# Turning P and dS: two sets of 64x64 products against one set of stacked K=128 products

## The chip, the cores and the metric

The kernel runs on one core of one Trainium2 chip. The metric is the device time of one execution in microseconds (us). Times are medians over several executions, with the lowest and highest; all runs named "fast" had a mean granted TensorE clock of 0.997 to 1.0 of full speed. "Slow" for this one-core program means over 1.5% above the fastest run of the same kernel. The experiments ran in three sets, each on another chip; the kernel before ran along in each.

## The reference

Forward and backward of window attention: 1024 windows of 8x8 = 64 tokens, 384 channels, one head of width 384.

```python
qkv = xw @ wqkv                                   # xw: 1024 windows x 64 x 384
p = softmax(einsum('bqc,bkc->bqk', q, k) * scale)  # P, 64 x 64 per window
o = einsum('bqk,bkc->bqc', p, v) @ wo
# returned: o and, for a given grad_out, the gradients of x, wqkv and wo
```

The backward pass needs dS, the gradient of the scores, and both P and dS also in transposed form.

## The kernel before

Work goes by "quads": 4 tiles of 128 tokens, each tile two windows, one in partitions 0 to 63 (LO) and one in 64 to 127 (HI). 128 quads make a software pipeline; in one step TensorE works on three of them. All PSUM tiles come from one ring of 8 banks, handed out in turn, so that a tile waits until the tile of eight hand-outs ago has been evicted.

```python
ring = ctx.enter_context(tc.tile_pool(name="ring", bufs=8, space=bass.MemoryType.PSUM))
...
def turn(st, kind):                 # kind 0: P -> PT, kind 1: dS -> ST
    n = ("PT", "ST")[kind]
    st[n] = dst = qp.tile([P, QUAD, WT], BF16, tag=n, name=n)
    pt = ring.tile([P, QUAD, WT], F32, tag="r", name="pt")
    for t in range(QUAD):
        for w, o, h in ((0, LO, HI), (1, HI, LO)):
            lhs, h = (st["Pb"][o, t, :], o) if kind == 0 else (st["ps"][h, w, t, :], h)
            nc.tensor.matmul(pt[o, t, :], lhsT=lhs, rhs=ident[h, h], start=True, stop=True)
    nc.vector.tensor_copy(out=dst[:], in_=pt[:])
...
def attend(st, pair, after=None):
    ...
    for t in pair:
        po, pu, pw, pd = [ring.tile([P, C], F32, tag="r", name=n) for n in ("po", "pu", "pw", "pd")]
        both((pu, "ST", "xq", True), (po, "PT", "uq", True))    # 4 products 64x64x384
        # osb <- po on ScalarE, Uq <- pu on VectorE
        both((pw, "Pb", "dq", True), (pd, "ST", "vq", False))   # 4 products 64x64x384
        # Wq <- pw on VectorE
        made.append((t, pd))
        store(out_0, osb, bp, t0 + t)
    if after is not None:
        turn(after, 0)
        turn(after, 1)
    for t, pd in made:
        for w, o in ((0, HI), (1, LO)):                          # K=128, M=64
            nc.tensor.matmul(pd[o, :], lhsT=st["ps"][:, w, t, :], rhs=st["tok"][:, :, t, w, :], start=False, stop=True)
        dsb = ob.tile([P, C], BF16, tag="d")                     # ob: 4 buffers of each kind
        # dsb <- pd on ScalarE, then store to out_1
```

A step (cut to the engine order of TensorE): scores, eight `uv` products, projection 0, one group `pg` of 12 weight-gradient products, `attend(c, (2, 3), b)` with the turn of quad b in it, projection 1 (its first products read `A_sb`), another `pg`, `attend(b, (0, 1))`. The matrix `ps` holds, for each tile and window, P in one half of the partitions and dS in the other: the stationary of the `pd` products. `xT`, `dT` and `tok` are transposed copies that DMA makes (of `x`, of the given gradient, and of the projections); their transposes are issued by SyncE, the loads of the gradient (`dq`) and the stores of `osb` and `dsb` by GpSimd, on one queue (q0 on the page, 151.68 MB).

## Time and profile before

| | before |
|---|---|
| time, median of the runs of the first comparison | 2078.51 us (2078.35 to 2081.12, 4 runs) |
| TensorE busy | 99% of the span |
| VectorE, ScalarE, GpSimd busy | 67, 71, 68% |
| turn products; their PSUM copies | 2048; 256 of 415 ns each |

Three lines of the profile page of the kernel before: the span, the busy time of the engines (us, share, number of instructions), and the shares by engine of the chain of work that ended last.

```profile
span 2076.4 us, 51332 instructions
PE 2057.4 (99%) x18814; PEld 1116.9 (54%) x18814; DVE 1391.1 (67%) x3235; ACT 1469.8 (71%) x3213; POOL 1418.0 (68%) x2566
...
PE 97%; DMA 2%; DVE 1%; ACT 0%; issue 0%
```

So only what shortens TensorE's stream shortens the kernel. The list of TensorE's waits in the same trace (total us, times, longest us) suggests that nothing is to be had from waits:

```profile
PE pt L74 <- DMA w_sb<-in_wqkv_dram: 6.5, 1, 6.5
PE pj L147 <- DMA dT<-dq: 2.2, 3, 1.0
PE pd L263 <- DMA tok<-yz: 1.7, 3, 0.8
```

That list is blind to short waits: a product of 384 columns is shown as 320 to 350 ns long, while the next of a plain sequence starts 162 ns after it. A wait of up to about 190 ns (350 less 162) fits under the bar of the product before. One has to look at starts. The timeline of one step of the kernel before, from the second tile's attention products to projection 1 (start us, duration us, engine, line, operation, shapes, count; weight loads and a few other lines left out):

```profile
1007.00 0.86 ACT L252 CAST osb<-po 128x384 bf16<-128x384 f32 x2 [0.16 <-ACT yz L150]
1007.06 0.32 PE L245 MATMUL pw<-dq,Pb 64*64 64x384 bf16 x1
1007.13 0.55 DVE L253 CAST Uq<-pu 128x384 bf16<-128x384 f32 x1
1007.27 0.35 PE L245 MATMUL pd<-vq,ST 64*64 64x384 bf16 x2
1007.28 0.35 PE L245 MATMUL pw<-dq,Pb 64*64 64x384 bf16 x1
1007.53 0.31 PE L230 MATMUL pt<-ident,Pb 64*64 64x64 bf16 x8
...
1007.74 0.31 PE L230 MATMUL pt<-ident,ps 64*64 64x64 bf16 x8
...
1007.98 0.52 PE L263 MATMUL pd<-tok,ps 128*64 128x384 bf16 x4
...
1008.42 0.82 PE L147 MATMUL pj<-xT,A_sb 128*128 128x512 bf16 x3
```

From the last attention product (1007.28) to the first turn product are 0.25 us instead of 0.16; the single instructions of the trace give 248 ns, and 42 ns before that start stands a semaphore update of ScalarE, some 10 ns after the end of the first `osb` copy (1006.995 + 0.479 = 1007.474). The second turn (1007.74) follows 42 ns after the update that comes, again some 10 ns late, with the end of the `Uq` copy (1007.133 + 0.548 = 1007.681). Both waits are for PSUM banks: the two turns take the banks of the first `po` and the first `pu`. Neither shows in TensorE's wait list, though they take 88 ns (248 less 160) and 61 ns of a step (the second turn starts 90 ns after the pair before it, where pairs follow after about 30). Over all steps the same lag of 42 ns repeats at the 5th, 25th and 50th percentile, as it must where that wait is the last to end. The start must also be later than the normal distance allows, as it is here (248 ns instead of about 160).

### The profile page before, as it was taken

To read this page: it belongs to the slowest core of one execution; us is meant where nothing else is said; L and a number is where in the kernel's file an instruction comes from. 1 tells how busy PE (TensorE), PEld (TensorE's weight loads), DVE (VectorE), ACT (ScalarE), POOL (GpSimd) and SP (SyncE) were. 2 spreads that over 40 slices of the span, in tenths; PEclk is the share of its full clock that TensorE was granted. 3 is DMA by queue.
4 is the path that set the end of the run, shared out by engine and by line. 5 is a ranking of instruction groups with operands and counts; after the bars stand their busy time and mean duration, and the time that the engine had idled before them with its cause. 6 is when DMAs were issued, how large, how long until landed. Compare 5 with 4: busy or idle time off the path is not lost.

```text
span 2076.4 us, 51332 instructions
## 1 busy us (share of the span) xinstructions
PE 2057.4 (99%) x18814; PEld 1116.9 (54%) x18814; DVE 1391.1 (67%) x3235; ACT 1469.8 (71%) x3213; POOL 1418.0 (68%) x2566
## 2 busy tenths in 40 slices
PE   8999999999999999999999999999999999999998
PEld 4455555555555555555555555555555555555554
DVE  5666666666666666666666666666666666666665
ACT  5767777777777777777777777677777777777773
POOL 4766766767667767667676766676767677666764
PEclk9999999999999999999999999999999999999999
DMA  9999999999999999999999999999999999999992
GB/s 203 222 210 199 200 200 197 213 197 199 199 197 201 201 201 201 200 197 201 199 198 197 205 199 194 198 209 194 203 199 203 203 192 202 199 200 198 201 172 77
DMA packets 997181, 409.06 MB, mean 197 GB/s; under 512 B 880704, under 2 KB 971584, under 8 KB 996928
## 3 DMA queue, kind: packets, MB, share of 16 engines
q1 hardware_dynamic: 873648, 253.80, 72.1%
q0 software_dynamic: 122880, 151.68, 30.7%
q8 instruction: 147, 2.41, 0.5%
q14 instruction: 106, 0.87, 0.1%
q10 hardware_dynamic: 400, 0.29, 0.0%
HBM read 101.84 MB, written 101.84 MB: 98 GB/s over the span
## 4 chain that ended last, share of the span: by engine, by line
PE 97%; DMA 2%; DVE 1%; ACT 0%; issue 0%
PE pg L278 24%; PE pj L147 24%; PE pj L219 23%; PE pd L263 5%; PE pu L245 5%; PE sd L165 5%; PE pw L245 4%; PE pd L245 3%; PE pt L230 3%; DMA tok<-yz 1%; DMA dT<-dq 0%; PE pc L96 0%; DMA w_sb<-in_wqkv_dram 0%; PE pe L369 0%; PE po L245 0%; PE pt L74 0%
## 5 line engine op out<-in xcount | busy, mean ns | idle before, releaser
L235 POOL DMA_DIRECT2D out_dram<-osb x1024 | 576.2, 569 | 432.0 <-ACT osb L252 338.1
L235 POOL DMA_DIRECT2D out_dram<-dsb x1024 | 570.6, 563 | 133.9 <-DMA dq<-in_grad_out_dram 38.8
L280 DVE TENSOR_TENSOR GF_acc<-pg,GF_acc 128x384 f32<-128x384 f32 x258 | 144.0, 558 | 489.1 <-PE pg L278 489.1
L278 PEld LDWEIGHTS <-xq 128*128 128x128 bf16 x3072 | 300.3, 98 | 225.4 <-issue 0.9
L219 PEld LDWEIGHTS <-xT 128*128 128x128 bf16 x3072 | 291.8, 98 | 182.2
L252 ACT CAST osb<-po 128x384 bf16<-128x384 f32 x512 | 220.9, 483 | 233.5 <-PE pu L245 162.3
L219 PE MATMUL pj<-B_sb,xT 128*128 128x384 bf16 x1536 | 333.4, 326 | 0.0
L219 PE MATMUL pj<-AT_sb,xT 128*128 128x384 bf16 x1536 | 333.3, 326 | 0.0
L118 POOL DMA_DIRECT2D dq<-in_grad_out_dram x512 | 273.8, 549 | 71.6 <-PE pj L147 27.3
L221 ACT CAST uq<-pj 128x384 bf16<-128x384 f32 x512 | 247.3, 483 | 74.4 <-PE pj L219 70.1
L253 DVE CAST Uq<-pu 128x384 bf16<-128x384 f32 x512 | 280.6, 548 | 8.4 <-PE pu L245 8.4
L266 ACT CAST dsb<-pd 128x384 bf16<-128x384 f32 x512 | 220.7, 482 | 89.6 <-PE pd L263 68.5
L255 DVE CAST Wq<-pw 128x384 bf16<-128x384 f32 x512 | 280.6, 548 | 0.0
L147 PE MATMUL pj<-dT,BT_sb 128*128 128x512 bf16 x1152 | 269.6, 379 | 2.2 <-DMA dT<-dq 2.2
L147 PE MATMUL pj<-xT,A_sb 128*128 128x512 bf16 x1152 | 270.8, 380 | 0.0
L278 PE MATMUL pg<-Uq,xq 128*128 128x384 bf16 x1536 | 270.4, 326 | 0.0
L278 PE MATMUL pg<-Wq,xq 128*128 128x384 bf16 x1536 | 270.0, 326 | 0.0
L221 ACT CAST vq<-pj 128x384 bf16<-128x384 f32 x512 | 250.0, 488 | 2.4
L152 ACT CAST yz<-pj 128x512 bf16<-128x512 f32 x384 | 224.7, 585 | 16.8
L245 PE MATMUL pw<-dq,Pb 64*64 64x384 bf16 x1024 | 227.2, 329 | 0.2
L198 ACT COPY ps<-Pb 64x256 bf16<-64x256 bf16 x256 | 103.3, 403 | 149.8 <-DVE Pb L195 148.3
L245 PEld LDWEIGHTS <-ST 64*64 64x64 bf16 x2048 | 119.9, 105 | 161.6 <-issue 148.5
(65 smaller groups left out, 2501.6 us busy)
## 6 DMA issues: line engine op xcount, KB each, us to landing
xq<-in_x_dram SPq DMA_DIRECT2D x512, 96.0 KB, 4.0
dq<-in_grad_out_dram POOLq DMA_DIRECT2D x512, 96.0 KB, 5.3
out_dram<-osb POOLq DMA_DIRECT2D x1024, 48.0 KB, 4.1
out_dram<-dsb POOLq DMA_DIRECT2D x1024, 48.0 KB, 4.0
dT<-dq SPq DMA_TRANSPOSE x128, 6.3
xT<-xq SPq DMA_TRANSPOSE x128, 7.3
tok<-yz SPq DMA_TRANSPOSE x128, 8.0
w_sb<-in_wqkv_dram SPq DMA_DIRECT2D x1, 864.0 KB, 5.7
```

The costliest lines, as they stand in the source:

```text
L118: nc.gpsimd.dma_start(out=dq[:, t, :], in_=dram_tile(grad_out, bp, t0 + t))
L147: nc.tensor.matmul(pj[:].rearrange("p t w k -> p (t w k)"), lhsT=wgt[:, m, mo * P:(mo + 1) * P], rhs=src[:, :, m, :], start=(m == 0), stop ...
L152: ENG[EV["y"][mo]](out=yz[:, mo, :, 1:3, :], in_=pj[:])
L219: nc.tensor.matmul(pj[:], lhsT=st["xT"][:, t, m, :], rhs=wgt[:, m, :], start=(m == 0), stop=(m == CK - 1))
L221: cp(out=dst[:, t, :], in_=pj[:])
L235: nc.gpsimd.dma_start(out=dram_tile(dst, bp, t)[WIN * w:WIN * (w + 1)], in_=src[h, :])
L245: nc.tensor.matmul(dst[o, :], lhsT=st[lhs][h, t, :], rhs=st[rhs][h, t, :], start=True, stop=done)
L252: ENG[EV["o"][t]](out=osb[:], in_=po[:])
L253: ENG[EV["U"][t]](out=st["Uq"][:, t, :], in_=pu[:])
L255: ENG[EV["W"][t]](out=st["Wq"][:, t, :], in_=pw[:])
L266: ENG[EV["d"][t]](out=dsb[:], in_=pd[:])
L278: nc.tensor.matmul(pw[:], lhsT=st["xq"][:, t, ma * P:(ma + 1) * P], rhs=st["UW"[f] + "q"][:, t, :], start=(i == 0), stop=(i == n - 1))
```

## The change

Both matrices lie stacked in `ps`, over all 128 partitions. One product of K=128 with the full 128x128 identity turns both at once and writes P-transposed and dS-transposed side by side: 8 products of 64x128 per quad instead of 16 of 64x64, one bank instead of two, one copy instead of two. The turn also moves behind the `pd` products, which work in the same 128x64 form.

```diff
--- before.py
+++ after.py
@@ -220,15 +220,19 @@
                              start=(m == 0), stop=(m == CK - 1))
         cp(out=dst[:, t, :], in_=pj[:])
 
-    def turn(st, kind):
-        n = ("PT", "ST")[kind]
-        st[n] = dst = qp.tile([P, QUAD, WT], BF16, tag=n, name=n)
-        pt = ring.tile([P, QUAD, WT], F32, tag="r", name="pt")
+    def turn(st):
+        pt = ring.tile([P, QUAD, 2, WT], F32, tag="r", name="pt")
         for t in range(QUAD):
-            for w, o, h in ((0, LO, HI), (1, HI, LO)):
-                lhs, h = (st["Pb"][o, t, :], o) if kind == 0 else (st["ps"][h, w, t, :], h)
-                nc.tensor.matmul(pt[o, t, :], lhsT=lhs, rhs=ident[h, h], start=True, stop=True)
+            for w, h in ((0, LO), (1, HI)):
+                nc.tensor.matmul(pt[h, t, :, :].rearrange("p s k -> p (s k)"), lhsT=st["ps"][:, w, t, :],
+                                 rhs=ident[:], start=True, stop=True)
+        st["PS"] = dst = qp.tile([P, QUAD, 2, WT], BF16, tag="PS", name="PS")
         nc.vector.tensor_copy(out=dst[:], in_=pt[:])
+
+    def turned(st, n, t, h):
+        if n in ("PT", "ST"):
+            return st["PS"][h, t, int((n == "ST") == (h == LO)), :]
+        return st[n][h, t, :]
 
     def store(dst, src, bp, t):
         for h, w in ((LO, 1), (HI, 0)):
@@ -242,7 +246,7 @@
         def both(straight, crossed):
             for h, o, (dst, lhs, rhs, done) in ((LO, LO, straight), (LO, HI, crossed), (HI, LO, crossed),
                                                 (HI, HI, straight)):
-                nc.tensor.matmul(dst[o, :], lhsT=st[lhs][h, t, :], rhs=st[rhs][h, t, :], start=True, stop=done)
+                nc.tensor.matmul(dst[o, :], lhsT=turned(st, lhs, t, h), rhs=st[rhs][h, t, :], start=True, stop=done)
 
         made = []
         for t in pair:
@@ -255,9 +259,6 @@
             ENG[EV["W"][t]](out=st["Wq"][:, t, :], in_=pw[:])
             made.append((t, pd))
             store(out_0, osb, bp, t0 + t)
-        if after is not None:
-            turn(after, 0)
-            turn(after, 1)
         for t, pd in made:
             for w, o in ((0, HI), (1, LO)):
                 nc.tensor.matmul(pd[o, :], lhsT=st["ps"][:, w, t, :], rhs=st["tok"][:, :, t, w, :], start=False,
@@ -265,6 +266,8 @@
             dsb = ob.tile([P, C], BF16, tag="d")
             ENG[EV["d"][t]](out=dsb[:], in_=pd[:])
             store(out_1, dsb, bp, t0 + t)
+        if after is not None:
+            turn(after)
 
     fill = []
 
@@ -317,8 +320,7 @@
         if c is not None:
             attend(c, (2, 3), b)
         else:
-            B(turn, 0)
-            B(turn, 1)
+            B(turn)
         for mo in range(CK):
             A(project, 1, mo)
         A(to_tokens)
```

## The prediction

> **What bounds the kernel.** TensorE's instruction stream. The page gives PE busy 99% at a full granted clock and 97% of the chain that ended last; DVE, ACT and POOL are at 67 to 71%. PE's wait list has only some 14 us. But matmul ends are modelled and overlap, so short waits count as "busy"; starts of single instructions show them. Products of N=384 follow each other after 162 ns, of N=512 after 216 ns. [...]

> **The part that changes**, once a step, 127 steps, medians or means of the trace, from the last start of the attention group to the first A_sb product:
> - attention to first turn product: 245 ns, where about 160 is normal. It starts 42 ns after a ScalarE semaphore update: the eviction of the first `po`, whose PSUM bank it reuses. About 88 ns lost.
> - first turn to second: 217 ns for eight products that take about 150 (pairs 30 ns apart). The second starts 42 ns after a VectorE update (`Uq` eviction of `pu`). About 61 ns lost.
> - second turn to `pd` products: 242 ns, 93 of it the change from 64x64 to 128x64 tiles.
> - `pd` to A_sb: 448 ns (two pairs 187 ns apart, the last followed after 258 = 163 + 95 for the change to the full array).
> Sum 1152 ns. [...]

> **After.** The number of mode changes stays (64x64, 128x64, full); the turn now runs in the 128x64 mode behind `pd`.
> - attention to `pd`: 277 ns, as before's other attention half shows.
> - `pd` to the turn: 190 + about 162 = 352 ns. No bank wait: the one bank was evicted some 0.4 us earlier.
> - turn: 8 products of N=128. The `pd` products show that the two column halves run as a pair (starts 3 to 4 ns apart)[...], plus 95 for the mode change: 319 ns.
> Sum 948 ns, so 0.20 us less a step, 26 us in all. Of that about 150 ns a step is the two bank waits, the rest fewer instructions.

> **Off the critical path.** VectorE: two copies of 415 ns become one; from 384 columns at 548 and 256 at 415, about 680 ns, so 19 us less in total, worth nothing. The banks that the next projection takes (`pu`, `pw`, `pd`) are evicted in time. The 56 ns wait of the second tile's `pd` for the GF_acc addition stays. DMA is nearly always busy, but its transposes land a median 9 to 12 us before use; at most 1 to 2 us of new DMA waits.

> **Prediction:** 2053 us (1.2% less), range 2046 to 2064. Faster by over 2%: 0.02; within 2%: 0.96; slower: 0.02.

> **What would show it.** Turn products 1024 instead of 2048[...]; no 90 ns gap with a 42 ns lag behind a semaphore; attention to A_sb about 0.95 us; VectorE about 20 us less busy.

> **What would make it wrong.** If the two column halves do not overlap when both stream the same identity, [...]the gain vanishes to about zero. If the bank waits only move (to A_sb's products or the next attention), half the gain goes. If DMA is tighter than its slack suggests, PE waits for `tok` or `dT`.

The sum of the forecast came to 277 + 352 + 319 = 948 ns. What is cut had its source outside the traces, and so had one term of the sum: the 224 ns (319 less 95) for the eight turn products. An estimate from the trace before comes close: products of 512 columns start 216 ns apart and products of 384 columns 162, so 128 columns are worth 54 ns; four pairs are 216 ns, and with 95 for the mode change 311 instead of 319. In the same trace the changes of tiling mode added 93 ns (second turn to `pd`), 95 (`pd` to `A_sb`: 258 less 163) and 115 (attention to `pd`: 277 less 162).

## The result, and the profile after

The changed kernel took 2059.92 us (2058.24 to 2064.11, 4 runs) against 2078.51 us: 18.6 us less. The ratio is 0.9911, with a 95% interval of 0.9893 to 0.9928; ratios are the mean time of one kernel's fast runs over that of the other's of the same rounds, so not quite the ratio of the medians quoted. By the 2% rule that is "same"; the direction is clear. The forecast of 2053 us was 6.9 us too low; the range of 2046 to 2064 held.

The same three lines of the page after the change:

```profile
span 2058.2 us, 49158 instructions
PE 2033.6 (99%) x17790; PEld 1109.3 (54%) x17790; DVE 1381.5 (67%) x3107; ACT 1468.8 (71%) x3213; POOL 1418.4 (69%) x2566
...
PE 93%; DMA 1%; ACT 1%; DVE 1%; POOL 0%; issue 0%; ACTq 0%; POOLq 0%
```

TensorE has 1024 products fewer, VectorE 128 copies fewer, as expected. New is that the chain lies on TensorE for 93% of the span, not 97%, and that the share of ScalarE rose from 0% to 1%. The section that the change rewrites, in the timeline of the changed kernel:

```profile
1002.23 0.35 PE L249 MATMUL pw<-dq,Pb 64*64 64x384 bf16 x1
1002.50 0.52 PE L264 MATMUL pd<-tok,ps 128*64 128x384 bf16 x4
1002.85 0.39 PE L227 MATMUL pt<-ident,ps 128*64 128x128 bf16 x8
1003.17 0.61 PE L147 MATMUL pj<-xT,A_sb 128*128 128x512 bf16 x2
```

Table 1 gives the medians over 126 steps, worked out from the starts of the single instructions (ns after the last attention product's start):

| | first turn product | first `pd` product | first `A_sb` product | predicted |
|---|---|---|---|---|
| before | 248 | 699 | 1147 | (1152 read) |
| after | 626 | 277 | 948 | 948 |

The mean over those steps fell from 1148 to 948 ns, 200 ns, or 25.2 us over 126 steps. **The local part of the forecast (0.20 us a step, 26 us) is right to within 1 us. But the kernel gained only 18.6 us.** The rest must have been given back elsewhere.

To find it, I compared each start-to-start distance on TensorE with the median of its kind and summed what was over by more than 80 ns ("irregular stalls"). Before: 9.4 us, of which 8.3 us in the first 100 us, 1.1 us at the end, none between. After: 16.8 us, of which 9.9 at the start, 1.0 at the end, and 6.0 us between 148 and 211 us, some 5 us of them in one episode from 204 us on. The difference of 7.4 us and the 25.2 us give 2076.4 - 25.2 + 7.4 = 2058.6 us, for a span of 2058.2 us.

The episode in the timeline of the changed kernel: first ScalarE's lines, then TensorE's (brackets: idle time before, and what ended it).

```profile
203.62 0.48 ACT L256 CAST osb<-po 128x384 bf16<-128x384 f32 x1 [2.10 <-DMA out_dram<-osb]
207.27 1.10 ACT L267 CAST dsb<-pd 128x384 bf16<-128x384 f32 x2 [3.18 <-DMA out_dram<-dsb]
```

```profile
204.15 0.65 PE L219 MATMUL pj<-AT_sb,xT 128*128 128x384 bf16 x3 [0.74 <-ACT osb L256]
204.63 0.65 PE L219 MATMUL pj<-B_sb,xT 128*128 128x384 bf16 x3
207.80 1.12 PE L219 MATMUL pj<-AT_sb,xT 128*128 128x384 bf16 x3 [2.52 <-ACT dsb L267]
```

ScalarE cannot write the next output tile, because the stores of its four buffers have not landed: the tile at 207.27 starts 100 ns after the store of the tile four before it landed (207.17). Until then ScalarE shows no other copy (3.18 us idle in the first fence), so banks stay full and TensorE stands still for 2.5 us. That store was late mainly because it was issued late. GpSimd's lines:

```profile
191.57 0.56 POOL L239 DMA_DIRECT2D out_dram<-dsb  x1 [1.79 <-DMA dq<-in_grad_out_dram]
200.43 2.22 POOL L239 DMA_DIRECT2D out_dram<-dsb  x4 [0.25 <-ACT yz L152]
```

The tile was ready at 187.07; its two stores were issued at 200.43 and 200.98, some 14 us later (median over the run: 3.4 us), and the second landed 6.2 us after that (median 4.2). GpSimd had fallen behind while it waited, among others at 191.57 for the landing of a `dq` load that it had issued eight DMAs before. Then comes a second bill, in the windows of the same stretch (us of the window; busy us and number of instructions per engine; granted clock, mean DMA share, GB/s):

```profile
200.00:205.00 5.00, 4.26 (x58) 2.35 (x56) 4.10 (x9) 1.30 (x3) 4.75 (x10) 1.00 1.16 184
205.00:210.00 5.00, 2.48 (x10) 1.05 (x9) 0.00 (x0) 2.56 (x7) 2.85 (x6) 0.74 1.11 249
210.00:215.00 5.00, 5.00 (x27) 2.66 (x26) 3.55 (x9) 3.81 (x10) 4.90 (x10) 0.92 0.96 193
```

The mean granted clock fell to 0.74 and 0.92 of full speed in these windows; products of 384 columns started 320 ns apart instead of 162, eight times in a row. The clock record of the trace shows half speed from 207.36 to 210.78 us. The clock dropped 2.4 us after the start of the last product before the stall (204.96). What makes it drop, and after how long a pause, this one episode does not show.

### The profile page after: what moved, and what is told of

Same layout as the page of the kernel before. It is cut to its first block, busy times and chain, and to the rows that moved or that the text cites. A ratio compares the mean times of both kernels' runs of the same rounds, so it can differ in the third digit from the quotient of the medians.

```text
span 2058.2 us, 49158 instructions
## 1 busy us (share of the span) xinstructions
PE 2033.6 (99%) x17790; PEld 1109.3 (54%) x17790; DVE 1381.5 (67%) x3107; ACT 1468.8 (71%) x3213; POOL 1418.4 (69%) x2566
## 2 busy tenths in 40 slices
DMA packets 997172, 408.92 MB, mean 199 GB/s; under 512 B 880704, under 2 KB 971584, under 8 KB 996928
## 4 chain that ended last, share of the span: by engine, by line
PE 93%; DMA 1%; ACT 1%; DVE 1%; POOL 0%; issue 0%; ACTq 0%; POOLq 0%
PE pg L281 24%; PE pj L147 23%; PE pj L219 23%; PE pd L264 5%; PE pu L249 5%; PE sd L165 5%; PE pw L249 4%; PE pd L249 3%; PE pt L227 1%; DMA out_dram<-dsb 1%; DMA tok<-yz 1%; POOL out_dram L239 0%; ACT uq L221 0%; ACT vq L221 0%; PE pe L371 0%
## 5 line engine op out<-in xcount | busy, mean ns | idle before, releaser
L249 PEld LDWEIGHTS <-PS 64*64 64x64 bf16 x3072 | 120.1, 105 | 163.6 <-issue 150.6
```

Source lines behind the costliest of these rows:

```text
L249: nc.tensor.matmul(dst[o, :], lhsT=turned(st, lhs, t, h), rhs=st[rhs][h, t, :], start=True, stop=done)
```

## The experiments

Two questions: (A) which part of the change makes the 200 ns, and (B) what took back the 7 us. All runs gave correct results, except the two with thin stores. Table 2 collects them, without the three runs with 8 output buffers, which are told below; "section" is the median of Table 1's third column, "saved" the difference of the mean section to before (1148) times 126 steps, "stalls" the irregular stalls of the profiled run, and "sum" is 2076.4 less saved plus the stalls above 9.4.

| kernel | section ns | saved us | stalls us: start, middle, end | sum | span of profiled run | time, median (range) |
|---|---|---|---|---|---|---|
| before | 1147 | 0 | 8.3, 0, 1.1 | 2076.4 | 2076.4 | 2078.51 (2078.35 to 2081.12) |
| after | 948 | 25.2 | 9.9, 6.0, 1.0 | 2058.6 | 2058.2 | 2059.92 (2058.24 to 2064.11) |
| e1_order | 994 | 19.4 | 9.2, 0, 0.9 | 2057.7 | 2058.6 | 2059.95 (2059.28 to 2060.80) |
| e2_stack_early | 948 | 24.5 | 8.2, 0, 0.9 | 2051.5 | 2052.2 | 2060.22 (2053.96 to 2064.72) |
| e7_early_two_banks | 1017 | 16.3 | 12.3, 0, 0.9 | 2064.0 | 2064.4 | 2066.12 (2063.95 to 2072.77) |
| e3_halves | 979 | 20.5 | 8.7, 10.4, 1.0 | 2066.6 | 2067.0 | 2060.47 (2059.72 to 2068.80) |
| e4_moved | 948 | 25.2 | 9.6, 0, 0.9 | 2052.3 | 2053.6 | 2056.00 (2055.32 to 2063.57) |
| e9_after_thin | 948 | 25.2 | 5.0, 0, 1.0 | 2047.8 | 2048.3 | 2050.17 (2049.84 to 2050.72) |
| e10_before_thin | 1146 | 0.1 | 5.6, 0, 1.0 | 2073.5 | 2073.4 | 2075.29 (2074.94 to 2075.55) |
| e11_early_group | 948 | 24.7 | 7.9, 11.3, 1.0 | 2062.5 | 2062.4 | 2062.48 (2057.88 to 2069.51) |

In all these rows the sum meets the span within 1.3 us: what a version costs is its section plus its irregular stalls (only e4_ob8, not in the table, with 39.1 us of stalls, misses by 3.3 us). The whole time alone would have ranked them wrongly, because runs of one kernel differ by up to 11.6 us (e11_early_group), and those of e2_stack_early by 10.8 us. The kernel before ran along with each set: 2079.06 us (7 runs) with e1, e2, e7 and e3; 2079.49 (11 runs) with the buffer runs; 2079.07 (11 runs) with e9 to e11.

### e1_order: the old products in the new place

```diff
-        if after is not None:
-            turn(after, 0)
-            turn(after, 1)
         for t, pd in made:
             ...
+        if after is not None:
+            turn(after, 0)
+            turn(after, 1)
```

> The kernel before, its 64x64 turn unchanged (16 products, two banks, two copies), but placed behind the pd products. Theory (the gain is the two hidden bank waits minus nothing else; tile-mode changes cost about 95 ns each): both bank waits (88 and 61 ns) go, but one more mode change comes (64x64, 128x64, 64x64, full array). Attention to A_sb: 277 + (190 + 160 + 95) + 150 + (119 + 29 + 95) = about 1115 ns against 1152 before and 949 after; time about 2074 us. Rival (the gain is the later place alone, because the waits are gone): attention to A_sb about 1000 ns or less and a time within 5 us of the changed kernel, 2060 to 2065 us.

The section took 994 ns and the kernel 2059.95 us. My theory of 1115 ns was wrong by 121 ns, and the rival held (about 1000 ns or less, and a time within 5 us of the changed kernel): by the whole time, e1 and the changed kernel (2059.95 and 2059.92 us) cannot be told apart. The extra mode change did come (`pd` to turn took 256 ns against 159 in the changed kernel), but I had charged the 16 products themselves far too high. The timeline shows why:

```profile
999.96 0.52 PE L260 MATMUL pd<-tok,ps 128*64 128x384 bf16 x4
1000.41 0.22 PE L230 MATMUL pt<-ident,Pb 64*64 64x64 bf16 x2
1000.44 0.22 PE L230 MATMUL pt<-ident,ps 64*64 64x64 bf16 x2
1000.46 0.20 PE L230 MATMUL pt<-ident,Pb 64*64 64x64 bf16 x2
1000.49 0.20 PE L230 MATMUL pt<-ident,ps 64*64 64x64 bf16 x2
...
1000.68 0.82 PE L147 MATMUL pj<-xT,A_sb 128*128 128x512 bf16 x3
```

Without the wait between them, products of the two turns mix: those from `Pb` and those from `ps` start in turn, 20 to 30 ns apart at first (in the program P turns within a half of the partitions, dS across; that this is why they can mix was not tested). All 16 started within 146 ns, where the kernel before needed 329 (248 to 577). From the first turn product to `A_sb` this old form took 271 ns, the new form 322. So the old products are not the slow part; the waits were.

### e2_stack_early: the new products in the old place

```diff
         made = []
         ...
+        if after is not None:
+            turn(after)
         for t, pd in made:
             ...
-        if after is not None:
-            turn(after)
```

> The changed kernel with its stacked turn put back in the old place, between the attention products and the pd products. Theory: the wait for the first po eviction (248 ns after the last attention product) hides behind the change to the 128x64 mode, which takes 277 ns anyhow, so the place does not matter: 277 + about 215 + 448 = 940 ns from attention to A_sb against 949 in the changed kernel; time 2056 to 2061 us. Rival (the later place is what removes the waits): the bank wait and the mode change add up, about 88 ns more, attention to A_sb about 1030 ns and about 2070 us.

The section took 948 ns again (mean 953): the place is worth nothing by itself. The first turn product starts 277 ns after the attention, where a plain `pd` product would, so the wait for `po` (over at 248 in the kernel before) hides behind the change to the 128x64 form. (In the traces of before, after and e1 such changes added 94 to 115 ns: 256 to 277 ns after a product of 384 columns instead of 162.) The theory holds. The times of its runs, 2053.96 to 2064.72 us, show how little the whole time says at this size.

```profile
1011.99 0.35 PE L249 MATMUL pw<-dq,Pb 64*64 64x384 bf16 x1
1012.26 0.41 PE L227 MATMUL pt<-ident,ps 128*64 128x128 bf16 x8
1012.51 0.49 PE L266 MATMUL pd<-tok,ps 128*64 128x384 bf16 x4
1012.93 0.39 PE L147 MATMUL pj<-xT,A_sb 128*128 128x512 bf16 x1
```

### e7_early_two_banks: the same, with a second bank

```diff
-        pt = ring.tile([P, QUAD, 2, WT], F32, tag="r", name="pt")
-        for t in range(QUAD):
+        for g in (0, 2):
+            pt = ring.tile([P, 2, 2, WT], F32, tag="r", name="pt")
+            for t in (g, g + 1):
                 ... (the products, into pt[h, t - g])
-        nc.vector.tensor_copy(out=dst[:], in_=pt[:])
+            nc.vector.tensor_copy(out=dst[:, g:g + 2], in_=pt[:])
```

> As e2_stack_early, but the turn in two PSUM banks of two windows each, with two copies. Theory: the second bank is that of pu, whose VectorE eviction ends some 410 to 450 ns after the last attention product, and the second half would be ready at 277 + 106 = 383: a wait of about 60 ns comes back, 1000 ns from attention to A_sb, about 7 us more than e2_stack_early. Rival (bank waits are not what limits, one bank or two is the same): the same as e2_stack_early within 2 us, no gap in front of the fifth product.

```profile
1004.01 0.35 PE L250 MATMUL pw<-dq,Pb 64*64 64x384 bf16 x1
1004.29 0.48 PE L229 MATMUL pt<-ident,ps 128*64 128x128 bf16 x8
1004.58 0.52 PE L267 MATMUL pd<-tok,ps 128*64 128x384 bf16 x4
1005.03 0.39 PE L147 MATMUL pj<-xT,A_sb 128*128 128x512 bf16 x1
```

From the first turn product to the first `pd` product are now 0.29 us instead of 0.25, and the section is 1017 ns, 69 more than with one bank; 1000 was expected. In the single starts the fifth product comes 97 ns after the pair before it (360 to 457), where with one bank it is 53 (360 to 413), and it starts 53 ns after the end of the `Uq` copy, as the second turn of the kernel before does. So the second bank brings back a wait.

The two waits of the kernel before do not simply add. In the trace of e6_before_ob8 (below), which leaves the turns as they were, the first `osb` copy ends 45 ns earlier, and the first turn product starts at 203 ns instead of 248; yet the second turn starts at 458 (457 before) and the section takes 1148 ns. In the old place the bank of `pu` alone sets the section; less of the first wait gains nothing by itself.

Together, e1, e2, e6 and e7 say: most of the gain (154 of 200 ns in e1) is the waits for PSUM banks. One can lose them by coming later (e1, at the price of a mode change, 256 ns instead of 159), or by asking for one bank only, whose wait is covered (e2).

What the old form would cost with no wait at all is open.

### e3_halves: the new products, one column half after the other

```diff
-        for t in range(QUAD):
-            for w, h in ((0, LO), (1, HI)):
+        for w, h in ((0, LO), (1, HI)):
+            for t in range(QUAD):
```

> The changed kernel with the turn's eight products issued four to the low column half, then four to the high one, in place of alternating. Theory (the alternating products run as pairs in the two column halves, which is what makes them cheap): products of one half follow each other after about 55 ns, so the turn takes about 400 to 430 ns in place of 224, and the time rises by about 0.2 us a step, some 25 us, to about 2080 to 2086 us. Rival (the products run one after the other anyway or the hardware pairs them whatever the order): no change, 2058 to 2062 us.

My theory fell. The section took 979 ns, 31 more, not some 200.

```profile
1009.43 0.52 PE L264 MATMUL pd<-tok,ps 128*64 128x384 bf16 x4
1009.79 0.42 PE L227 MATMUL pt<-ident,ps 128*64 128x128 bf16 x8
1010.13 0.61 PE L147 MATMUL pj<-xT,A_sb 128*128 128x512 bf16 x2
```

### e4_ob8, e4_moved, e6_before_ob8, e8_early_ob8: more output buffers

Now question B. First theory: four output buffers are too few.

```diff
-    ob = ctx.enter_context(tc.tile_pool(name="ob", bufs=4))
+    ob = ctx.enter_context(tc.tile_pool(name="ob", bufs=8))
...
-    GFb = setup.tile([P, 2, CK, C], BF16, tag="GFb")
-    GFT = setup.tile([P, 2, CK, C], BF16, tag="GFT")
+    GFb = qp.tile([P, 2, CK, C], BF16, tag="tok", name="GFb")
+    GFT = qp.tile([P, 2, CK, C], BF16, tag="yz", name="GFT")
```

The second hunk only makes room; e4_moved is the changed kernel with that hunk alone, e6 applies both to the kernel before, e8 to e2_stack_early.

> The changed kernel with 8 output buffers of each kind in place of 4 (two tail tiles moved to other pools to make room). Theory (the missing 7 us are stalls in which ScalarE waits for an output buffer whose store has not landed, and TensorE then for a bank and after it for its clock): the stall near 200 us goes, ScalarE's waits for out_dram stores go from 70 us to near 0, the sum of irregular TensorE stalls from 16.8 to about 11 us, time 2053 to 2055 us, and runs agree within 1 us (2058.2 to 2064.1 before). Rival (DMA itself is full and the wait only moves to tok, dT or xT): within 2 us of the changed kernel, TensorE's waits for DMA grow by 4 us or more.

> Control: the changed kernel with the two tail tiles moved to other pools, but still 4 output buffers. All theories: as the changed kernel, 2058 to 2064 us, stalls as there.

> The kernel before with 8 output buffers of each kind. Theory: it has no store stall that reaches TensorE (its irregular stalls, 9.4 us, are in the first 75 us and the last 40), so nothing is gained: 2077 to 2079 us. The gain of the change would then be measured free of that stall: e6 to e4 24 to 26 us. Rival (the kernel before pays for stores as well): 2070 to 2075 us.

> The stacked turn in the old place with 8 output buffers: candidate for the fastest. Theory: as e4_ob8 within 2 us, 2051 to 2055 us. Rival (late place matters): 10 us slower than e4_ob8.

The theory of too few buffers fell. With 8 buffers the changed kernel took 2055.61, 2086.04, 2086.68, 2091.91, 2093.50 and 2113.39 us; e8 ran 2056.09 to 2097.87 us. Four of the six runs of e4 and three of the six of e8 were slow (2086.04 us lies just under the line), so I claim no size for the loss; but no gain shows. e6 gave 2078.70 us (ratio 0.999, interval 0.9973 to 1.0006), so the kernel before does not care, apart from one slow run of 2115.76. The control e4_moved took 2056.00 us (2055.32 to 2063.57): three of its four runs lie below the 2058 to 2064 us that I expected, and its profiled run lacks the episode near 200 us. It ran in another set than the changed kernel, so whether the moved tiles or only the chance of the episode make the 4 us is open. In the profiled run of e4_ob8 (2086.04 us) the waits had moved, as the rival said. TensorE's waits there:

```profile
PE pd L264 <- DMA tok<-yz: 18.8, 13, 2.9
PE pj L147 <- DMA dT<-dq: 7.8, 12, 1.7
```

The median time from issue to landing of the `tok` transposes rose from 8.3 to 11.0 us. Against the same two lines after the change (4.1 us and 1.2 us) this is worse. The traces show where it came from. In e4_ob8 the second store of a tile was issued a median of 16 us (`osb`) and 18 us (`dsb`) after the tile was ready; in the changed kernel it was 1.6 and 3.4 us, in e6 1.6 and 2.6. One reading, worked out from these numbers: more buffers let ScalarE run further ahead of GpSimd, and the `dq` loads stand in the same queue of GpSimd as the waiting stores. SyncE, which waits for `dq` before it issues the transposes, first after the change, then in e4_ob8:

```profile
SPq L127 <- DMA dq<-in_grad_out_dram: 10.6, 6, 3.8
SPq L127 <- DMA dq<-in_grad_out_dram: 278.7, 120, 4.8
```

So the order on GpSimd's queue is a strong suspect; no run tested it, for example with the loads on another queue. Why one run of six escaped (2055.61 us) stays open.

### e9_after_thin and e10_before_thin: less for DMA to move

Second theory: DMA itself is near its limit, so take load away and change nothing else. Each store keeps its place and its semaphore, but moves 8 tokens in place of 64. The outputs are wrong.

```diff
-            nc.gpsimd.dma_start(out=dram_tile(dst, bp, t)[WIN * w:WIN * (w + 1)], in_=src[h, :])
+            nc.gpsimd.dma_start(out=dram_tile(dst, bp, t)[WIN * w:WIN * w + 1], in_=src[h.start:h.start + WIN, :])
```

> The changed kernel with every store cut to one eighth of its rows, the number of stores unchanged (wrong result on purpose), to take load from the DMA engines alone. Theory (the part of the gain that is missing is stalls from late DMA: a first part in the first 100 us, 8 to 12 us in all kernels, and episodes of 6 to 10 us in the middle of some runs): the episodes in the middle vanish, stalls at the start shrink by half; time 2046 to 2053 us, runs within 1.5 us of each other. Rival (the episodes come from the order on the issuing queues, not from DMA load): 2055 to 2064 us with the same spread.

> The kernel before with the same thin stores (wrong result on purpose). Theory: it has the stalls at the start only, which shrink: 2072 to 2076 us; the difference to e9 is then the 25 us that the changed section gives by its own starts, within 2 us. Rival: 2078 to 2081 us as before, and a difference to e9 of 18 to 19 us as in the full kernels.

The changed kernel took 2050.17 us with runs within 0.9 us of each other, the kernel before 2075.29 us. The difference is 25.1 us, which is what the section gives by its own starts ((1147 - 948) ns times 126 steps = 25.1 us). No episode in the middle was left, and TensorE's wait list of e9 no longer names `tok`, and `dT` with 0.2 us only. Its bytes, on the page of e9:

```profile
DMA packets 964404, 320.38 MB, mean 156 GB/s; under 512 B 864320, under 2 KB 955200, under 8 KB 964160
```

In the changed kernel it was 408.92 MB at 199 GB/s. So the missing gain was lost to stores that were late, and to what waited behind them: light stores are worth 9.8 us to the changed kernel (2059.92 to 2050.17) and 3.2 to 3.8 us to the kernel before (2078.51 or 2079.07 to 2075.29); the full changed kernel was not run again in the set of e9. Which limit it is (bytes, packets, or the order and pace of GpSimd's queue) these runs do not separate. Thin stores also land sooner (a median of 3.1 and 2.6 us, from 4.5 and 4.2), and GpSimd is busy 129 us less (1289.1 from 1418.4 us), so its queue keeps up: a tile waited at most 5.8 us for the issue of its stores, in the changed kernel up to 14.0 us.

### e11_early_group: more TensorE work in the first steps

All kernels lose 5 to 12 us in the first 100 us, where the `pg` products are still missing and steps are short. The candidate closes the first group of weight-gradient products after one quad.

```diff
-            if held and (len(held) == GQ or i == n):
+            if held and (len(held) == (1 if i == 1 else GQ) or i == n):
```

> Candidate: the changed kernel, in which the first group of the weight-gradient products holds one quad in place of three, so that the products that fill the steps begin one step after the first quad, not three. Theory (the first steps are short of TensorE work, run ahead of DMA, and stall there for 8 to 10 us for tok and dT): stalls in the first 100 us shrink to about 4 us, 2053 to 2056 us. Rival (the start is a matter of latency, work moved there just adds): no change or 1 us slower for the added group.

It did not pay: 2062.48 us (2057.88 to 2069.51). The stalls at the start fell from 9.9 to 7.9 us in the profiled run, but 11.3 us of stalls stood between 160 and 220 us, where the changed kernel and e3_halves have theirs too. No version here beats the changed kernel by more than the spread of its runs.

## Why the prediction was right or wrong

The range and the direction were right; the gain was 18.6 us of the 25.5 predicted (2078.5 less 2053).

- "Attention to A_sb about 0.95 us": right, 948 ns predicted, 948 measured. Each term held: attention to `pd` 277, `pd` to the turn 349 (352 predicted), turn to `A_sb` 322 (319 predicted).
- "No bank wait: the one bank was evicted some 0.4 us earlier": right, and e2 shows that it would have held in the old place too.
- "Of that about 150 ns a step is the two bank waits, the rest fewer instructions": the sum came out, the parts did not. e1 has all 2048 products and still saves 154 ns, though it pays for one more mode change; it even runs its turn faster (271 against 322 ns to `A_sb`). The wait for `pu` cost more than its visible 61 ns: it also kept the two turns from mixing (16 starts in 146 ns in e1, in 329 before). The 88 ns for `po` are worth nothing while the wait for `pu` stands (e6). The new form's own merit is that it fits the mode of its neighbours (159 ns from `pd` to the turn, 256 in e1) and needs one bank.
- "The `pd` products show that the two column halves run as a pair": right, starts 3 ns apart, 53 to 56 ns between pairs. Eight products one after the other (448 ns at 56 each), the case in which the forecast saw no gain, did not come, not even when the halves were issued one after the other (e3).
- "Two copies of 415 ns become one ... about 680 ns, so 19 us less in total": the copy took 677 ns, but VectorE's busy time fell by only 9.6 us (1391.1 to 1381.5). In the step shown the second old copy started 331 ns after the first, so 84 ns of each pair overlapped and was counted once; 128 times (746 - 677) is 8.8 us. It cost nothing.
- **The step that failed: "DMA is nearly always busy, but its transposes land a median 9 to 12 us before use; at most 1 to 2 us of new DMA waits."** That term measured 7.4 us in the profiled run. A median of the slack said nothing of the rare late one (the 5th percentile for `dT` was about 3 us before, 1.7 us after), and the transposes were the wrong place to look: the largest single loss came through the stores, from a GpSimd that issued them some 14 us late, over their four buffers, ScalarE and the PSUM banks to TensorE, with a slower clock as an after-effect. e9 and e10 show that with lighter stores the forecast difference appears in full (25.1 us). That the time still fell into the range is in part luck: how large an episode a run meets was not forecast, runs of the changed kernel differ by 5.9 us, and one of the four (2064.11 us) lies just outside the range.

## What to carry to other kernels

A TensorE that is 99% busy can still wait (here 88 and 61 ns in each step): look for starts that come later than the normal distance and follow a semaphore update at one constant small lag, and count the PSUM banks that the tiles before still hold. A rewrite of a product can be worth most for the bank that it does not ask for (the old products without the bank waits already saved 154 of the 200 ns) and for the tiling mode that it shares with its neighbours (159 ns from `pd` to the turn instead of 256). Part of a saving on the bounding engine can come back as rare, uneven stalls (here 7.4 of 25.2 us), so account for a run as section plus stalls, and test a suspected limit by taking load away, not only by adding buffers. Of an output that is late, ask first when its store was issued (here some 14 us after the tile was ready).
